# A new order of all steps, and new PSUM pairs, for a fused recurrence and feed-forward kernel on one core

## The chip, the cores and the metric

The kernel runs on one core of one Trainium2 chip. The metric is the time of one execution in microseconds of device time (us); lower is better. The kernel before was run three times: 1061.87, 1062.71 and 1066.75 us, so its median is 1062.71 us.

## What is computed

The reference is a recurrence over 768 time steps for 4 x 8 heads of size 40, whose output goes through an RMS normalisation and a gated feed-forward layer. All tensors are float32.

```python
for t in range(S):                                   # S = 768, state is 40 x 40 per head
    y[:, :, t] = einsum('bhd,bhde->bhe', r[t], state)
    Sa = einsum('bhde,bhe->bhd', state, a[t])
    state = state * w[t][:, :, None, :] - einsum('bhd,bhe->bhde', Sa, b[t])
    state = state + einsum('bhd,bhe->bhde', v[t], k[t])
x = y as (3072 tokens, 320)
xn = x / sqrt(mean(x * x) + 1e-6) * rms_g
out = (silu(xn @ w_gate) * (xn @ w_val)) @ w_out     # 320 -> 1536 -> 320
```

## The kernel before

The time axis is cut into 24 **chunks** of 32 steps. Each chunk has three stages. `front` (L652) loads the chunk's six inputs, turns them with TensorE, and builds products inside the chunk, level by level (1, 2, 4, 8, 16 steps), in eight PE steps that follow each other through ScalarE (ACT) and VectorE (DVE). `inverse` (L760, and `early_inverse`, L778, for the first four chunks) solves a triangular system on VectorE, in some 60 short instructions, with a round trip through DRAM on either side. `main` (L810) carries the state from chunk to chunk and makes the chunk's output. After every second chunk `feed` (L939) runs one **group** of 256 tokens, 12 groups in all, through the feed-forward layer in 12 slices of the hidden dimension. Its weights come from DRAM again for each group: each slice is one load into one of five buffers `wf`, and a buffer comes free only when the `out` matmuls of the slice that used it are done. Group 0 needs the weights in a narrowed form, which `narrow` (L973) makes in 24 half slices at the start of the kernel, with ScalarE, VectorE and DMAs.

No engine call is made where the stages are written. `Plan.add` (L280) notes each step as a piece with its engine, the pieces that it needs, and the PSUM **room** that it uses. There are 6,028 pieces: 2,858 for DVE, 1,024 for ACT, 905 for PE, 696 for SP (all of them DMA issues) and 545 for POOL (GpSimd; 460 of them DMA issues). A PE piece is 3 to 64 matmul records in the profile. `Plan.issue` (L322) then issues the pieces in the order that the string `ORDER` (L33) gives. A word of it is a number counted from the first piece that has not been issued yet, and a `-` is a **filler**: one 128x128 matmul on the identity (L1015) whose result nobody reads. The string `PAIRS` (L228) says which of three PSUM pairs (two banks each) each of the 499 rooms gets. A room keeps its pair from its first to its last piece, so a pair that is given to a new room also makes that room's first matmul wait for the last reader of the old one. The order is the program's: each engine runs its own pieces in this order and waits at each for what the piece needs. DMA issues stand in it too; the loads of chunks 1 to 23 are issued by POOL, weights, chunk round trips and outputs by SP.

The profile knows most instructions by the line of a helper: L444 is every VectorE operation on tensors, L464, L467 and L470 those of ScalarE, L479 and L476 fills and copies on POOL, L483 every DMA issue, L486 every matmul, L489 every turn (transpose by TensorE) and L1015 the fillers. PE steps carry these names below: `turn`, `gramk` (products inside a chunk), `lower`, `state`, `update`, `score`, `level`, `y0` (stage `main`), and `h64`, `h`, `out` (stage `feed`).

## Time and profile before

| | |
|---|---|
| median of three runs | 1062.71 us |
| the profiled execution: span from first to last instruction | 1060.6 us |
| runs' median less that span | 2.1 us |
| PE busy | 1009.5 us (95%), 23406 matmuls |
| weight loads on PE (they overlap matmuls) | 829.3 us |
| DVE busy | 842.3 us (79%), 2861 instructions |
| ACT busy | 468.1 us (44%) |
| POOL busy | 309.5 us (29%) |
| fillers on PE (302 records, two for each of 151) | 48.0 us |
| DMA | 143.35 MB, 135 GB/s on average |

The profile is one execution on the chip. Busy time is time in which an engine runs an instruction; a gap before an instruction is put down to what ended it. The chain of waits (the work that ended last, followed back from the end) is PE for 72% of the span, DVE for 8% and DMA for 4%.

### The profile page before, as it was taken

Reading aid. Unit: us, or ns where it says so; the run is one execution under the profiler, and the core shown is the slowest. Engines: PE = TensorE matmul, PEld = TensorE weight load, DVE = VectorE, ACT = ScalarE, POOL = GpSimd, SP = SyncE. Lnnn points to the kernel's source line nnn. Section 1 sums busy time; section 2 is a strip of 40 time slices with the busy share of each in tenths; the row PEclk is TensorE's granted clock in tenths of the full one; section 3 lists DMA queues with packets and bytes.
Section 4 is the critical chain, followed back from the end, with each engine's and each line's share of the span. In section 5 each row is a group of like instructions: output and inputs, shape, how many; then the busy total and the mean of one; then the engine's idle time right before and its main releaser. Section 6 shows DMA issues by size and latency. Waiting matters only on the chain.

```text
span 1060.6 us, 53494 instructions
## 1 busy us (share of the span) xinstructions
PE 1009.5 (95%) x23406; PEld 829.3 (78%) x23406; DVE 842.3 (79%) x2861; ACT 468.1 (44%) x1043; POOL 309.5 (29%) x554
## 2 busy tenths in 40 slices
PE   7868999999999999999999999999999999999997
PEld 6767777777888778787778778787777888787875
DVE  8978878776868988898898798989889899787411
ACT  6856666643543534434443444434344443431211
POOL 8824413120532241241233241340331331110000
PEclk9777998999999999999999999999999999999999
DMA  9965458766565483655565555574555555443252
GB/s 168 216 155 133 77 127 207 211 123 178 127 140 126 106 173 96 150 134 125 123 155 129 135 132 114 122 160 119 137 126 126 138 137 138 100 132 102 80 162 68
DMA packets 172457, 143.35 MB, mean 135 GB/s; under 512 B 125504, under 2 KB 143872, under 8 KB 172224
## 3 DMA queue, kind: packets, MB, share of 16 engines
q1 hardware_dynamic: 153856, 116.96, 42.9%
q0 software_dynamic: 16192, 22.64, 12.1%
q8 instruction: 184, 3.01, 1.2%
q10 hardware_dynamic: 2176, 0.33, 0.3%
q14 instruction: 49, 0.40, 0.1%
HBM read 123.86 MB, written 15.99 MB: 132 GB/s over the span
## 4 chain that ended last, share of the span: by engine, by line
PE 72%; DVE 8%; DMA 4%; ACT 3%; issue 3%; POOL 2%; SPq 1%; DVEq 0%; ACTq 0%; POOLq 0%
PE ps L486 50%; PE po L486 13%; PE ps L489 8%; DMA wf<-sW 2%; DVE LT L444 1%; DVE y L444 1%; DVE tmp L444 1%; POOL kbn L483 1%; DVE Yi L444 1%; DVE K L444 1%; SPq L483 1%; DMA sY<-Yi 1%; ACT VU L467 1%; PE po L1015 0%; DVE Ab L444 0%
## 5 line engine op out<-in xcount | busy, mean ns | idle before, releaser
L486 PE MATMUL ps<-xg,wf 128*128 128x256 f32 (+1 forms) x1728 | 353.5, 390 | 4.0 <-DVE xg L444 2.0
L486 PEld LDWEIGHTS ps<-xg,wf 128*128 128x128 f32 (+1 forms) x1728 | 261.4, 188 | 57.2 <-issue 15.0
L486 PE MATMUL po<-wf,hT 128*128 128x320 f32 x576 | 183.1, 449 | 0.1
L464 ACT ACTIVATE sg<-ps 128x256 f32<-128x256 f32 x144 | 53.6, 382 | 228.2 <-PE ps L486 224.9
L444 DVE TENSOR_TENSOR tmp<-Yi,M 128x60 f32<-128x60 f32 (+24 forms) x620 | 130.7, 211 | 19.1 <-DMA M<-sB 5.9
L444 DVE TENSOR_TENSOR Yi<-Yi,tmp 128x60 f32<-128x60 f32 (+24 forms) x620 | 129.7, 209 | 12.7
L483 POOL DMA_DIRECT2D VU<-in_v_dram x92 | 53.2, 584 | 274.1 <-PE ps L486 141.8
L486 PEld LDWEIGHTS po<-wf,hT 128*128 128x128 f32 x576 | 102.5, 191 | 35.7 <-issue 4.1
L444 DVE TENSOR_TENSOR hT<-ps,sg 128x256 f32<-128x256 f32 x144 | 59.7, 420 | 67.2 <-ACT sg L464 66.4
L444 DVE TENSOR_TENSOR K<-K,T 128x512 f32<-128x512 f32 (+1 forms) x192 | 93.4, 496 | 8.3 <-PE ps L486 5.8
L486 PEld LDWEIGHTS ps<-Ab,K 40*64 40x64 f32 x4608 | 77.2, 138 | 28.1 <-issue 10.5
L467 ACT COPY K<-K 128x256 f32<-128x256 f32 (+1 forms) x168 | 71.7, 443 | 58.4 <-PE ps L486 39.2
L486 PE MATMUL ps<-Ab,K 40*64 40x56 f32 x4608 | 87.2, 224 | 9.7 <-issue 3.8
L444 DVE TENSOR_TENSOR As<-ps,msi 128x256 f32<-128x256 f32 (+1 forms) x186 | 78.9, 476 | 14.4 <-PE ps L486 13.8
L467 ACT COPY KN<-ps 128x640 f32<-128x640 f32 x96 | 66.1, 690 | 53.5 <-PE ps L489 23.3
L483 POOL DMA_DIRECT2D kbn<-in_b_dram x92 | 53.3, 583 | 96.7 <-PE ps L486 94.3
L486 PEld LDWEIGHTS ps<-As,KN 128*40 128x40 f32 x3072 | 66.5, 124 | 15.7 <-issue 10.4
L483 POOL DMA_DIRECT2D kbn<-in_k_dram x92 | 53.6, 585 | 82.7 <-PE ps L486 82.6
L486 PE MATMUL ps<-As,KN 128*40 128x32 f32 x3072 | 73.2, 205 | 3.1 <-issue 2.5
L483 POOL DMA_DIRECT2D wn<-in_w_dram x92 | 51.6, 567 | 62.7 <-DVE tmp L444 24.1
L444 DVE TENSOR_TENSOR y<-y,ps 128x256 f32<-128x256 f32 x119 | 50.0, 420 | 16.2 <-PE ps L486 13.7
L444 DVE COPY_PREDICATED LT<-near,ps 128x384 f32<-128x384 uint32 (+2 forms) x72 | 52.2, 725 | 2.6 <-PE ps L486 2.0
(133 smaller groups left out, 1546.0 us busy)
## 6 DMA issues: line engine op xcount, KB each, us to landing
wf<-sW SPq DMA_DIRECT2D x144, 480.0 KB, 3.9
M<-sB SPq DMA_DIRECT2D x80, 128.0 KB, 4.1
rn<-in_r_dram SPq DMA_DIRECT2D x24, 160.0 KB, 5.4
sW<-ex SPq DMA_DIRECT2D x16, 240.0 KB, 3.4
out_dram<-o SPq DMA_DIRECT2D x48, 80.0 KB, 4.2
kbn<-in_k_dram POOLq DMA_DIRECT2D x92, 40.0 KB, 3.9
kbn<-in_b_dram POOLq DMA_DIRECT2D x92, 40.0 KB, 4.1
wan<-in_a_dram POOLq DMA_DIRECT2D x46, 80.0 KB, 4.9
```

What stands on the lines that cost most here:

```text
L444: plan.add("DVE", kind, lambda at: fn(at(o), *m(at)), [o], aps(*args))
L464: plan.add("ACT", "act", lambda at: nc.scalar.activation(at(o), at(a), f, **kw), [o] + aps(acc), [a])
L467: plan.add("ACT", "copy", lambda at: nc.scalar.copy(at(o), at(a)), [o], [a])
L483: plan.add(by, "dma", lambda at: queue.dma_start(out=o, in_=i), [o], [i])
L486: return o, lhsT, rhs, lambda at: nc.tensor.matmul(at(o), lhsT, rhs, start=start, stop=stop, skip_group_check=True)
L489: return o, i, ident, lambda at: nc.tensor.transpose(at(o), i, ident)
```

## The change

Only the two strings differ; every piece, its instruction and its operands are the same, and so are the numbers of pieces (6,028), fillers (151) and rooms (499). The new `ORDER` and `PAIRS` come from a search by local exchanges that judged an order by the mean of three draws in which transfers land late.

```diff
 ORDER = """
-85 83 84 76 58 78 86 74 73 59 60 75 5 89 61 88 77 4 43 6 201 7 87 334 90 44 8 214 213 53 62 9 - - - - - - - - 93 18 10
...
+86 5 4 6 7 - 8 9 10 11 12 13 14 15 16 17 58 59 43 19 - 20 - 25 18 38 42 76 85 83 79 73 74 84 75 78 87 77 88 93
+94 - 95 96 100 101 108 111 21 557 558 559 124 112 - 22 26 113 23 24 121 125 568 577 566 578 588 569 589 567
...
 PAIRS = """
-0120112210001221012012210211000102102120201021100221210111012202202000111100112120100012102221212201000112001120122221
...
+01201021120012121120211201020000012020101000212222212101110101200020001111011121202222100200122222011221010121
...
```

Read as orders of each engine, the two differ nearly everywhere, but seldom by much. If the pieces of an engine are laid end to end with the durations of the trace of before, a DVE piece stands 3.6 us of DVE work away from its old place on average, an SP piece 2.7, an ACT piece 2.3 and a POOL piece 4.3. Which stages follow each other, and which chunk runs beside which group, is as before, and both orders end in the same four `out` steps. The three pairs serve 179, 166 and 154 rooms before and 164, 169 and 166 after.

## The prediction

> **What bounds the kernel now.** I read the page's rows of busy time and of the 40 slices first, then busy time by stretch, then the waits of PE, then stretches of the timeline.

> ```profile
> PE 1009.5 (95%) x23406; PEld 829.3 (78%) x23406; DVE 842.3 (79%) x2861; ACT 468.1 (44%) x1043; POOL 309.5 (29%) x554
> ...
> PE   7868999999999999999999999999999999999997
> ...
> DVE  8978878776868988898898798989889899787411
> ...
> PEclk9777998999999999999999999999999999999999
> ```

> The slices are 26.5 us each. From the seventh on PE is full. Before that neither PE nor its clock is. Stretches of busy time give sizes (length, PE, PEld, DVE, ACT, POOL, granted clock, DMA share, GB/s):

> ```profile
> 0.00:20.00 20.00, 14.18 (x246) 13.55 (x250) 15.65 (x48) 9.76 (x19) 18.60 (x43) 1.00 1.00 176
> 20.00:40.00 20.00, 14.78 (x344) 12.61 (x336) 18.62 (x40) 17.92 (x37) 17.46 (x39) 0.82 0.84 174
> 40.00:60.00 20.00, 18.42 (x360) 16.68 (x362) 19.66 (x71) 17.16 (x36) 11.30 (x22) 0.76 0.88 205
> 60.00:80.00 20.00, 13.24 (x354) 11.80 (x347) 13.37 (x47) 9.21 (x19) 2.98 (x7) 0.76 0.67 163
> 80.00:100.00 20.00, 17.64 (x653) 15.85 (x655) 16.95 (x58) 10.70 (x23) 8.74 (x16) 0.73 0.55 146
> 100.00:160.00 60.00, 56.20 (x1734) 47.67 (x1733) 47.32 (x137) 39.28 (x88) 21.29 (x39) 1.00 0.50 100
> 160.00:200.00 40.00, 38.28 (x843) 31.64 (x842) 33.90 (x119) 27.87 (x60) 8.68 (x15) 0.91 0.76 205
> 200.00:600.00 400.00, 390.48 (x9071) 317.25 (x9063) 327.70 (x1143) 169.81 (x388) 122.44 (x209) 1.00 0.58 138
> 600.00:1000.00 400.00, 391.18 (x9460) 320.15 (x9458) 337.51 (x1177) 157.79 (x357) 97.48 (x167) 1.00 0.53 126
> ```

> There are two regimes. Up to 100 us PE is idle for 21.7 us, while DVE is the busy one between 20 and 60 (38.3 of 40) and POOL before 40 (36.1 of 40). From 200 to 1000 PE is busy 781.7 of 800 us: the steps that PE does there set the end, and an order can gain only what PE loses between steps. All PE idle time there is 18.3 us, so large gains are out of reach.

> How PE's time depends on order shows in the timeline (start, length, operation):

> ```profile
> 726.84 1.89 PE L486 MATMUL ps<-xg,wf 128*128 128x256 f32 x8
> 728.66 0.83 PE L486 MATMUL ps<-VU,KN 64*40 64x40 f32 x64
> 729.29 1.12 PE L486 MATMUL ps<-rE,vut 40*64 40x32 f32 x64
> 730.23 1.14 PE L486 MATMUL ps<-Ab,K 40*64 40x56 f32 x64
> 731.30 0.92 PE L489 MATMUL ps<-ident,ST 104*104 104x104 f32 x8
> ```

> A step counts from its start to the next start. An `h` step (first row) takes 1.82 us here, ahead of a step whose weights have another shape; ahead of one of its own shape the least is 1.73. `gramk` (fourth row) takes 1.07 ahead of a turn and 0.97 ahead of `update`. I call such a change of shape a switch.

> **The change part by part.** Nothing is added or removed, so each term is a count from the two orders times a size from this trace.

> *Switches.* Sorted by shape (full 128 rows with turns; `h64`; 64x64; `level`; `lower`; `state`), neighbours on PE differ 532 times before and 497 times after; from group 1 on, where PE is the bound, 414 and 381. Over all pairs after 200 us, a step ahead of a switch takes 0.121 us more than its least, one without 0.063 (stalls over 0.5 us left out). So 33 fewer switches are 33 x 0.058 = 1.9 us; by the least values (0.10) 3.3. I take **-2.0**; ends 0 (the wait merely moves) and -3.3.

> *Short leads.* For each PE step I took the PE work between it and the earlier PE step whose result reaches it through other engines (a freed PSUM pair counted too), less the measured durations of those other steps. Before, of 759 steps from group 1 on, 16 have a lead under 0, 135 under 1 us, 254 under 3, 354 more. Their measured lateness is 0.417, 0.080, 0.035 and 0.052 us each, 44.9 in all. After, the counts are 2, 120, 252 and 385: 0.8 + 9.6 + 8.8 + 20.0 = 39.2, so 5.7 less. But 18.4 us fall on steps with leads over 3 us, late for another reason (queues of DVE and ACT, which the new order mixes anew). I take **-3.5**; ends 0 and -5.7.

> *Weight loads.* A load waits for the `out` step that frees its buffer, so its lead is the PE work from there to the slice's first matmul.

> ```profile
> DMA to landing us min/median/max: 2.0/4.0/9.3
> ```

> Leads under 5 us fall from 4 to 1 and the shortest grows from 3.9 to 4.8; those under 10 rise from 27 to 33. At the median landing all are covered: 0. If the six added short leads met the slowest landing they would cost at most 6 x (9.3 - 4.8) = 27 us, in practice a fraction; this goes to the range.

> *Fillers.* The count is the same, but 8 of the 151 move behind group 0, where PE has no time to spare: 8 x 0.22 = 1.8 us unless they stand in a wait. I take **+0.9**.

> *The start.* POOL is the queue to look at. The last load of chunk 1's k and b stood behind 15.9 us of POOL work and was issued at 17.7; now fills and copies that were needed later stand ahead of it, and it is behind 27.1, so it is issued at 28.9. It lands 3.9 us later by the median row, 6.4 by its own case:

> ```profile
> kbn<-in_k_dram POOLq DMA_DIRECT2D x92, 40.0 KB, 3.9
> ```

> So it lands at 32.8 to 35.3; turn, copy and `gramk` (1.08 + 1.0 + 1.16) give 36.0 to 38.5, where DVE by its own order wants the result at 34.0. DVE waits 2.0 to 4.5 us, and its whole queue with it. Against that stand 1.4 us that DVE idled there anyway, and an order that ends the first elimination 1.8 us of DVE work sooner: net -1.2 to +1.3 at 60 us. Behind that the DVE order brings main of chunk 0 3.8 us forward on average, the `hT` that feeds group 0's eighth `out` 3.8 and chunk 5's `front` 2.8. I take **-1.5** (ends -4 and +5, the latter for a wait of 4.5 that nothing gives back). The chunk 0 loads and round trips on SP move by 1 us on average, and the load that the first elimination waits for is 6 us of SP's order earlier: nothing. The tail is the same: nothing.

> Sum: -2.0 - 3.5 + 0.9 - 1.5 = **-6.1 us**. The span of 1060.6 becomes 1054.5; with the 2.1 us that lie between the profiled span and the runs' median, 1056.6.

> **The rivals.**

> 1. *No change.* Stalls change places: DVE, at 0.83 busy from 200 on, gets a new queue order, and its lateness (18.4 us on steps with long leads) grows by what the short leads give. For it: the weight loads' leads, on which late transfers act, have not grown. Against it: the counts of short leads fall in each class. Time: switches alone, less the fillers, 1061.6.

> 2. *A colder, later start; slower than before.* The granted clock is 0.73 to 0.82 from 20 to 100 us, and a `gramk` that takes 1.16 us at full clock takes 1.98 at half. The new order has 104 fillers rather than 111 ahead of group 0, none rather than 3 (and a `lower`) between chunk 1's first and second `gramk`, and 2 rather than 11 just ahead of the first `inv` step, where PE already idles 4.2 us. If the half clock lasts on through 100 to 160 us, where PE is busy 56.2 of 60, each microsecond of it loses half: 36 us more at half clock cost 18, and the time is 1062.7 - 6.1 + 18 = 1075. It decides against the kernel once more than 23 us are added (11.4 us lost, 1068). Against it: the clock was low between 80 and 100, where PE had 17.6 of 20 busy, so fillers do not govern it alone. [...]

> 3. *More.* Start and short leads give their full ends: -3.3 - 5.7 + 0 - 4 = -13, or 1049.7.

> **How the numbers follow.** Forecast 0.50, at 1056.6, reaching from 1052 to 1062; no change 0.20; slower start 0.18; more 0.12. I take 0.5% (5.3 us, limits 1057.4 and 1068.0) as what a measurement can tell from no change. Faster: 0.30 of the forecast's 0.50 and all of the 0.12, 0.42. Within: 0.20 of the forecast and 0.17 of the first rival, 0.37. Slower: 0.18 and 0.03, 0.21. The range reaches from 1048 (below rival 3) to 1070: it leaves out most of rival 2 and little else. The forecast's own range is 1052 to 1062.

> **What would show it.** PE busy from 200 to 1000 nearer to its clean sum, and the same work ended earlier: group 1's last `out`, 308 us before, should end at 305 or less, and from there to the end another 3 to 5 us should be gained. On POOL the load named above lands at 33 to 35 us and DVE waits ahead of chunk 1's first masked copy. It would be wrong if groups 1 to 11 take as long as before, if a weight load ends many PE waits, or if the granted clock is low past 100 us.

## The result and the profile after

The changed kernel took 1131.07 us (median of four runs, 1123.89 to 1137.86) against 1062.29 us for the kernel before beside it: a ratio of 1.0625, 95% interval 1.0549 to 1.0701. So it is 69 us slower where the prediction said 6 us faster. The profiled execution took 1137.86 us, its span is 1136.1. Now and then a run lies over 1.5% above the fastest of its kernel; in what follows it counts in the median and not in the ratio.

The page of the kernel after: busy time, and PE, DVE and the granted clock in 40 slices of 28.4 us.

```profile
PE 1036.5 (91%) x23406; PEld 849.6 (75%) x23406; DVE 843.9 (74%) x2861; ACT 459.7 (40%) x1043; POOL 309.6 (27%) x554
...
PE   6878887998998999899999899998989999998998
...
DVE  7878676856867787788888789867878879886321
...
PEclk8779997999998999999999999999989999999999
```

PE's row is no longer full from the seventh slice on; eights stand between the nines to the end. The clock dips as late as the 30th slice. DVE is busy for as long as before (843.9 and 842.3 us), so the same work takes longer: something holds PE up. The same stretches as in the prediction (length, PE, PEld, DVE, ACT, POOL, granted clock, DMA share, GB/s):

```profile
0.00:20.00 20.00, 11.66 (x182) 10.73 (x182) 16.50 (x45) 10.66 (x19) 18.04 (x47) 1.00 0.83 174
20.00:40.00 20.00, 14.25 (x276) 13.46 (x280) 14.09 (x34) 12.60 (x26) 14.26 (x28) 0.79 0.65 142
40.00:60.00 20.00, 16.91 (x366) 15.36 (x358) 19.24 (x62) 15.22 (x33) 9.07 (x18) 0.70 0.76 168
60.00:80.00 20.00, 15.30 (x416) 13.98 (x418) 17.27 (x62) 11.26 (x25) 5.05 (x11) 0.73 0.77 209
80.00:100.00 20.00, 17.02 (x557) 15.33 (x549) 11.63 (x37) 11.49 (x22) 6.39 (x14) 0.84 0.43 91
100.00:160.00 60.00, 53.07 (x1688) 44.82 (x1687) 44.62 (x140) 38.41 (x88) 20.57 (x37) 0.97 0.43 94
160.00:200.00 40.00, 32.39 (x626) 26.32 (x628) 27.49 (x89) 17.30 (x36) 11.92 (x21) 0.83 0.63 164
200.00:600.00 400.00, 372.72 (x8530) 303.96 (x8522) 308.37 (x1068) 163.49 (x378) 109.17 (x184) 0.97 0.53 129
600.00:1000.00 400.00, 377.82 (x8991) 307.87 (x8995) 328.46 (x1149) 153.96 (x360) 109.55 (x187) 0.97 0.50 123
```

From 200 to 1000 us PE is busy 750.5 us, before 781.7, and it does 17,521 matmuls there, before 18,531. The last `out` of group 0 ends at 254.6 us (before 238.7), of group 1 at 332.5 (308.4), of group 6 at 764.4 (711.5), of group 11 at 1131.3 (1055.1). So 16 us are lost by group 0 and some 5.5 us in each group behind it: no single place.

What ends PE's idle time (engine, line, tile; total us, times, longest), before and then after:

```profile
PEld ps L486 <- issue: 62.4, 157, 2.0
...
PE ps L486 <- issue: 16.9, 25, 1.8
```

```profile
PEld ps L516 <- issue: 94.9, 167, 3.8
...
PE ps L516 <- issue: 38.0, 39, 3.6
```

"issue" is idle time for which the profile shows no cause, neither a semaphore nor a DMA. It has grown most. On the timeline of PE after (start, length, operation, idle time ahead of it) it looks like this:

```profile
394.73 0.73 PE L516 MATMUL ps<-Ab,K 40*64 40x56 f32 x33
397.44 0.69 PE L516 MATMUL ps<-Ab,K 40*64 40x56 f32 x31 [1.99 <-issue]
398.06 1.99 PE L516 MATMUL ps<-xg,wf 128*128 128x256 f32 x8
```

This is one `gramk` step of chunk 9, 64 matmuls on the same two tiles, broken for 2 us between its 33rd and its 34th matmul. Nothing that the profile sees (a semaphore, a DMA, another engine) ends the wait.

What can, by these traces, is the supply of instructions. The row of the DMA queues is the same in both kernels but for the share, 1.2% before (queue, kind, packets, MB, share):

```profile
q8 instruction: 184, 3.01, 1.1%
```

Each packet has 16384 bytes. PE's part of the trace holds some 47,150 instructions (a matmul record comes with a weight load; 335 are waits on semaphores), which is about 184 times 256. That makes 64 bytes for each, and the packets come from 17.7 to 1118.6 us of the span (before 15.6 to 1043.7): PE's own program is brought in while it runs, in **blocks** of 256 instructions. A block is 128 matmul records with their weight loads, or two `gramk` steps. Numbered from the first instruction in the trace, the long waits without a cause lie at one and the same place of these blocks: of 51 gaps over 0.75 us between the starts of weight loads after 200 us, 22 (36.6 us) end with instruction 190 to 198 modulo 256, nearly all at 193 or 194. Before it was 9 of 21 (10.3 us), at the same two numbers. I call this place the **cut**. The gaps elsewhere have grown as well, from 12 with 11.5 us to 29 with 38.5.

The packets tie the gaps at the cuts to the supply. Of the 22 gaps there, 21 end 1.2 to 1.6 us after a packet of this queue has come in; of the 29 gaps elsewhere, only two do. The n-th packet starts 1.1 (before) and 1.3 us (after) behind the n-th cut in the median, and in neither trace does PE pass the next cut before that packet has come in: the least distance from its end to that cut is 1.2 us before and 0.9 after.

**The theory**, read from these two traces: behind a cut PE has one block in hand, asks for another, and must have it before the first is used up. Where PE waited over 0.75 us at a cut after 200 us, the cut ahead lay 3.1 to 6.0 us back (5% to 95%; median 4.7; 31 waits in the two kernels). Small steps use up a block faster: two `gramk` steps take 1.9 us. For each block I sum the clean durations of its steps and count what it lacks to 3.6 us, the **shortfall**: 14.9 us over all blocks after 200 us before, 31.9 after. The 3.6 us are the median in the trace of before from the start of a packet to the use of its block (3.8 after). They hold time in which a block lay ready, so they are a scale and not a measured limit; the medians from a cut to its packet (1.1), of the packet (1.1) and from its end to the end of a long gap (1.4) happen to add up to the same. The rivals: late transfers with the weights' leads, the queue orders of DVE and ACT, and the start with its fillers and clock.

To size it, I compared every interval between weight loads after 200 us with the clean duration of its step. The excess is *cut* (over 0.2 us, at instruction 190 to 198), *others* (over 0.2 us at a step's start, where its last operand from DVE, ACT or a DMA has just come) or *rest* (changes of shape, half clock, small things):

| us after 200 us | before | after | difference |
|---|---|---|---|
| cut | 14.4 | 41.2 | +26.8 |
| others | 19.1 | 35.9 | +16.8 |
| rest | 15.4 | 35.3 | +19.9 |
| sum | 48.8 | 112.3 | +63.5 |

The clock is in the rest: before it is never at half between 200 us and the end of the last `out`, after it is for 51.2 us in twelve stretches. Nine of them stand behind waits at a cut, three (at 236.5, 478.9 and 1048.9 us) behind gaps of 2.7 to 3.3 us elsewhere.

### The profile page after: what moved, and what is told of

Its sections match the earlier page's. It is cut to its first block, busy times and chain, and to the rows that moved or that the text cites. A ratio compares the mean times of both kernels' runs of the same rounds, so it can differ in the third digit from the quotient of the medians.

```text
span 1136.1 us, 53417 instructions
## 1 busy us (share of the span) xinstructions
PE 1036.5 (91%) x23406; PEld 849.6 (75%) x23406; DVE 843.9 (74%) x2861; ACT 459.7 (40%) x1043; POOL 309.6 (27%) x554
## 4 chain that ended last, share of the span: by engine, by line
PE 67%; DVE 15%; issue 6%; DMA 5%; ACT 3%; POOL 2%; SPq 1%; DVEq 0%; ACTq 0%; POOLq 0%
PE ps L516 45%; PE po L516 12%; PE ps L519 8%; DVE LT L474 2%; PE po L1045 2%; DVE tmp L474 2%; DVE Yi L474 2%; DVE K L474 2%; POOL kbn L513 2%; DVE y L474 2%; SPq L513 1%; DVE Ab L474 1%; DMA M<-sB 1%; DVE hT L474 1%; DMA sB<-LT 1%
## 5 line engine op out<-in xcount | busy, mean ns | idle before, releaser
L516 PE MATMUL ps<-xg,wf 128*128 128x256 f32 (+1 forms) x1728 | 363.0, 402 | 0.9 <-DVE y L474 0.9
L516 PEld LDWEIGHTS ps<-xg,wf 128*128 128x128 f32 (+1 forms) x1728 | 268.4, 195 | 54.2 <-issue 15.1
L516 PE MATMUL po<-wf,hT 128*128 128x320 f32 x576 | 185.5, 456 | 5.9 <-issue 3.9
L516 PEld LDWEIGHTS po<-wf,hT 128*128 128x128 f32 x576 | 106.9, 198 | 41.4 <-issue 8.3
L516 PE MATMUL ps<-Ab,K 40*64 40x56 f32 x4608 | 89.7, 227 | 25.1 <-issue 9.3
L516 PEld LDWEIGHTS ps<-Ab,K 40*64 40x64 f32 x4608 | 79.7, 140 | 42.8 <-issue 20.6
L474 DVE TENSOR_TENSOR As<-ps,msi 128x256 f32<-128x256 f32 (+1 forms) x186 | 80.3, 475 | 19.7 <-PE ps L516 18.1
L516 PEld LDWEIGHTS ps<-As,KN 128*40 128x40 f32 x3072 | 65.4, 124 | 21.3 <-issue 13.9
L503 POOL TENSOR_TENSOR ss<-ss,mhalf 128x1 f32<-128x1 f32 x24 | 16.2, 674 | 189.5 <-DVE ss L474 188.6
```

Of the source, the lines that this page charges most:

```text
L474: plan.add("DVE", kind, lambda at: fn(at(o), *m(at)), [o], aps(*args))
L503: plan.add("POOL", "tt", lambda at: nc.gpsimd.tensor_tensor(o, a, b, op), [o], [a, b])
L516: return o, lhsT, rhs, lambda at: nc.tensor.matmul(at(o), lhsT, rhs, start=start, stop=stop, skip_group_check=True)
```

## The experiments

**Instructions put ahead of an unchanged order.** A filler is split into two of half the width: the same columns, but four more instructions (two matmuls of two records, each with a weight load, in place of one). The cuts move through the whole program; apart from the split fillers themselves, all of them ahead of group 0, nothing else does. The number of split fillers is 32, 4, 36, 16, 48, 16 and 52 in the seven runs.

```diff
-    plan.warm = lambda: nc.tensor.matmul(po_[:, 0, DM:DM + P], ident, ident, start=False, stop=False, skip_group_check=True)
+    filler = lambda lo, hi: nc.tensor.matmul(po_[:, 0, DM + lo:DM + hi], ident, ident[:, lo:hi], start=False, stop=False, skip_group_check=True)
+    def warm():
+        fillers[0] += 1
+        for lo, hi in ((0, 64), (64, P)) if fillers[0] <= 32 else ((0, P),):
+            filler(lo, hi)
+    plan.warm = warm
```

> The kernel before, with its first 32 fillers each issued as two of 64 columns in place of one of 128: the same order everywhere and the same columns of work, but 128 more instructions in TensorE's stream (a matmul is four: two passes of a weight load and a matmul) ahead of group 0. Theory (TensorE starves for instructions): the traces show TensorE's stream fetched in packets of 16384 bytes (184 of them in both kernels, 256 instructions each), a median of 3.6 us from asking for one to its use, and the stalls of both kernels at one and the same place of these blocks (instruction 193 of 256). Blocks of small matmuls are used up in less than 3.6 us of clean time; after 200 us these shortfalls add up to 14.9 us in the kernel before and 31.9 us in the kernel after. Moved by 128 instructions the blocks of the kernel before are cut elsewhere, and the shortfalls add up to 33.6 us: so 30 to 75 us slower (1090 to 1135), with most of the loss inside TensorE steps. Rivals (fillers and clock at the start, late transfers, pairs and order of VectorE and ScalarE): nothing of theirs is changed, so 1060 to 1068.

> The kernel before, with its first 4 fillers each issued as two of 64 columns: 16 more instructions ahead of group 0. Theory: the shortfalls of the blocks add up to 14.4 us after 200 us in place of 14.9, so the time stays within 6 us of the kernel before (1057 to 1068). Together with the run of 128 it tells whether the place of the blocks matters or any change of the fillers. Rivals: the same, 1060 to 1068.

> The kernel after, with its first 36 fillers each issued as two of 64 columns: 144 more instructions ahead of group 0. Theory: the shortfalls of its blocks add up to 43.3 us after 200 us in place of 31.9, so slower still than after, by 10 to 40 us (1140 to 1170). Rivals: as the kernel after, 1124 to 1138.

> The kernel before with its first 16 fillers each issued as two of 64 columns: 64 more instructions ahead of group 0, the order unchanged. The shortfalls of the blocks below 3.6 us after 200 us are 27.5 us at this place, against 14.9 at the kernel's own and 33.6 at 128 (which took 1117). Theory (the place of the cuts): 1090 to 1115. Rival (128 was unlucky, the order is robust): 1060 to 1080.

> The kernel before with its first 48 fillers each issued as two of 64 columns: 192 more instructions, the order unchanged. Shortfalls 31.7 us. Theory: 1095 to 1120. Rival (128 was unlucky): 1060 to 1080.

> The kernel after with its first 16 fillers each issued as two of 64 columns: 64 more instructions, the order unchanged. Shortfalls 40.1 us, against 31.9 at its own place and 43.3 at 144 (which took 1154). Theory: 1125 to 1155; the changed order is slow at every place. Rival (after's own place is unlucky): below 1100.

> The kernel after with its first 52 fillers each issued as two of 64 columns: 208 more instructions, the order unchanged. Shortfalls 35.9 us. Theory: 1120 to 1150. Rival (after's own place is unlucky): below 1100.

Measured (the ratio is to the kernel before on the same chip, 1066.2 to 1066.6 us there; the kernels' own places head the two halves):

| order, instructions ahead | shortfall | us | ratio, 95% interval | cut | others | rest |
|---|---|---|---|---|---|---|
| before, 0 | 14.9 | 1062 to 1067 | 1 | 14.4 | 19.1 | 15.4 |
| before, 16 | 14.4 | 1077.5 | 1.0099 (1.0065 to 1.0134) | 13.7 | 18.6 | 15.9 |
| before, 64 | 27.5 | 1105.0 | 1.0363 (1.0303 to 1.0424) | 38.8 | 18.7 | 22.2 |
| before, 128 | 33.6 | 1116.6 | 1.0479 (1.0413 to 1.0545) | 42.0 | 20.5 | 38.7 |
| before, 192 | 31.7 | 1113.2 | 1.0433 (1.0375 to 1.0492) | 44.4 | 20.0 | 27.5 |
| after, 0 | 31.9 | 1131.1 | 1.0625 (1.0549 to 1.0701) | 41.2 | 35.9 | 35.3 |
| after, 64 | 40.1 | 1145.7 | 1.0740 (1.0670 to 1.0810) | 48.2 | 36.4 | 41.0 |
| after, 144 | 43.3 | 1154.1 | 1.0760 (1.0661 to 1.0860) | 48.2 | 36.2 | 40.0 |
| after, 208 | 35.9 | 1145.7 | 1.0708 (1.0612 to 1.0804) | 42.0 | 36.3 | 45.0 |

Six of the seven came out within the theory's range and outside the rivals'. For the kernel after this says less, since the intervals of its ratios at the three new places overlap with that at its own. The waits of the kernel before with 128 instructions ahead (the same two rows):

```profile
PEld ps L486 <- issue: 91.0, 169, 3.5
PE ps L486 <- issue: 39.7, 35, 3.4
```

With an order that has not changed in any queue, they have the size of the kernel after, and they still begin at 193 and 194 of a block, so at other steps. The column "others" hardly moves with the place (18.6 to 20.5 and 35.9 to 36.4): it belongs to the order. The miss is 16 instructions: after 200 us the loss is as expected (48.3 us, before 48.8), but group 0 ends at 250.2 us instead of 238.7. The start is sensitive too (251.3, 255.0 and 247.8 with 64, 128 and 192), and the shortfall, counted after 200 us, does not cover it. Whether the cuts or the split fillers delay the start was not told apart.

**The supply alone.** A kernel that only issues matmuls: 8 sets of 4 large ones, 80 steps of the shape of `gramk`, 40 large sets, and 80 steps again, with 60 loads of 480 KB running beside their first part. It was run once.

```diff
+        gramk(80)
+        large(40, xg)
...
+        for load in range(60):
...
+            nc.sync.dma_start(out=wf[load % 5].bitcast(I32), in_=src[load % 2 * P:load % 2 * P + P, 960 * (load % 3):960 * (load % 3) + 960])
+        gramk(80)
```

> Leaves the reference's work out: it only issues matmuls, and writes zeros. 80 steps of the shape of gramk (32 small matmuls, 128 instructions) with nothing else running, then 40 sets of 4 large ones, then 80 steps of gramk while SP loads 60 tiles of weights. Theory: clean, a step of gramk takes 0.97 us, so a block of 256 instructions 1.9 us, and 80 of them 78 us; if a block can't be had faster than every 3.6 us, the run of gramk takes about 140 us with a stall in each block, and longer or not while the loads run (the fetch's share of the queues). If only latency counts and several fetches may be under way, about 78 us. Rivals need 78 us in both.

Three stretches: small matmuls alone, with the loads, and behind them (length, PE, PEld, DVE, POOL, clock, DMA share, GB/s):

```profile
60.00:100.00 40.00, 39.09 (x1403) 37.87 (x1400) 0.00 (x0) 0.00 (x0) 0.50 0.02 5
260.00:300.00 40.00, 25.10 (x884) 23.88 (x880) 0.00 (x0) 0.00 (x0) 0.50 1.02 404
320.00:360.00 40.00, 39.47 (x1408) 38.08 (x1405) 0.00 (x0) 0.00 (x0) 0.50 0.02 5
```

128 matmul records with their weight loads are a block, so a block takes 40 x 128 / 1403 = 3.65 us alone and 40 x 128 / 884 = 5.8 us beside full DMA queues, with 2.1 to 2.9 us of it waited at instruction 193 of each block (3.9 in the first). No instruction here depends on the loads. The first 80 steps took 146.7 us, near the theory's 140, but the clock stood at half, at which PE by itself needs nearly that (it was busy for 39.09 of 40 us): a match by luck, and 3.65 us is only an upper bound for the idle machine. The clock had fallen to half at 23.7 us, at the end of a gap of 2.7 us at a cut. It stayed there for 146.8 us, though PE was busy for 39.1 of 40, and came back at 170.5 us, 4.9 us after the large matmuls had begun. The 5.8 us is the supply's own: at the same clock PE was idle for 14.9 of 40 us beside 404 GB/s, and for 0.9 beside 5 GB/s.

**Less traffic.** The reloads of the weights are left out from the 18th on, in both kernels, so later groups multiply by old weights.

```diff
-                dma(wf, sW[f + e])
+                dma(wf, sW[f + e], skip=FT * g + f + e >= FT + WB)
```

> The kernel after without the reloads of the weights: the first 17 loads of wf (group 0, and one for each of the five tiles) stay, the other 127 are left out, so the later groups multiply by old weights; every other instruction and order stays. It takes some 62 of the 117 MB off SP's queue. Theory: a block of instructions took 3.65 us with the queues empty and 5.8 us with them full where the fetch was run alone, so with less traffic fewer blocks run out: the waits at instruction 193 after 200 us fall from 41 to 15 to 25 us, and the time to 1085 to 1115. Rival, late transfers of weights as the cause of the loss: down to the kernel before or below, at most 1070, with the same waits at instruction 193. Rival, other engines' orders or the clock: 1120 to 1138.

> The kernel before without the same 127 reloads of weights (left out as in the run of after). Theory: its 14 us of waits at instruction 193 after 200 us fall to about 7, so 1040 to 1060; the gap between the two kernels shrinks from 69 to 35 to 60 us. Rival, late transfers of weights as the cause: 1062 and a gap near nothing.

After fell to 1095.25 us (1.0301, 1.0227 to 1.0376), before to 1060.48 (0.9939, 0.9905 to 0.9973): the gap is 35 us. The rows of waits of the kernel after without reloads:

```profile
PEld ps L516 <- issue: 73.8, 147, 5.2
...
PE ps L516 <- issue: 21.3, 24, 5.1
```

Cut fell from 41.2 to 16.8, rest from 35.3 to 16.7 (half clock 10.2 us), others stayed (36.6). Before: 11.4, 16.3 and 20.2; its waits at cuts fell less than expected (to about 7), and its time lies at the edge of the theory's range. So late weights were not what held the kernel after: without them its waits for others are as they were. What fell with the traffic were the waits at cuts and the half clock, and half of the 69 us goes with them.

**TensorE's order rearranged.** Steps of PE are exchanged within a few places so that no block is short; judged by a model with the trace's durations and the supply of instructions. The first, second and fourth change PE's order alone, the third those of all engines. A piece of the first, as PE's steps in order, named by stage, number and kind (an excerpt):

```diff
 main9.turn
+feed3.out
 front11.gramk
+feed3.h64
+feed3.h
 main9.y0
-feed3.h64
 main9.score
-feed3.h
```

> The kernel after with TensorE's order alone rearranged: 459 of its 905 steps move, most by one place and none by more than seven, so that no block of 256 instructions is made of small steps only; the orders of the other four queues, the pairs, the fillers and the start stay those of the change. The shortfalls of TensorE's blocks below 3.6 us after 200 us fall from 31.9 to about 9 us, and the shape switches rise from 470 to 517. Theory (TensorE starves for instructions): most of the loss comes back, 1035 to 1080. Rivals: a cause in the orders of VectorE, ScalarE, POOL or SP, in the pairs, or in the fillers and the start is untouched, so 1115 to 1140; a loss by switches or leads of TensorE's own would grow.

> The kernel before with TensorE's order alone rearranged in the same way: 404 of its 905 steps move, most by one place and none by more than nine. The shortfalls of its blocks fall from 14.9 to about 6 us; shape switches 512 to 523. Theory: faster than the kernel before by 10 to 40 us (1022 to 1055), since the kernel before also starves in places. Rivals: the kernel before doesn't starve, so 1055 to 1075.

> The kernel before with the orders of all five engines moved by local exchanges, judged by when TensorE's blocks run out beside the waits for other engines (439 steps of TensorE by at most eight places). The shortfalls fall from 14.9 to about 7 us. Theory: faster than the kernel before by 10 to 40 us (1022 to 1055), about like the rearranged TensorE order alone. Rivals: what moves on the other engines decides, so as likely slower than the kernel before as faster.

> The kernel before with TensorE's order alone rearranged (451 steps, by at most ten places) so that blocks are not short wherever they are cut: the shortfalls are 8 to 22 us over all places of the cuts, against 15 to 35 in the kernel before, at the price of 39 more shape switches (512 to 551). Theory: 1035 to 1065, and little change if instructions are put ahead of it. Rivals: slower by the switches alone, 1062 to 1075.

| run | us | ratio, 95% interval | cut | others | rest |
|---|---|---|---|---|---|
| after, PE rearranged | 1151.2 | 1.07 (two runs), no interval | 16.7 | 65.9 | 40.0 |
| before, PE rearranged | 1122.7 | 1.0546 (1.0468 to 1.0624) | 20.9 | 53.3 | 32.2 |
| before, all rearranged | 1251.0 | 1.1748 (1.1655 to 1.1840) | 21.3 | 122.2 | 51.9 |
| before, for any place | 1140.2 | 1.0709 (1.0639 to 1.0780) | 19.7 | 64.2 | 22.3 |

All four missed, and the third agrees with its rival, that what moves on the other engines decides. The first did what it was made for at the cuts, and the time did not come back: PE now waits for results. The rows of its waits:

```profile
PEld ps L488 <- issue: 63.0, 145, 2.5
PEld ps L488 <- ACT K L469: 16.3, 22, 1.8
...
PE ps L488 <- issue: 16.6, 18, 2.4
```

The issue rows are back at the size of before, and a wait for ACT of 16.3 us stands beside them (4.2 in the kernel after). In the kernel before, the rearranged orders did not even lower the cut: 20.9 and 19.7 for 14.4. So the shortfall tells what moving the cuts does to a given order; it did not tell which order would be good. And the leads for other engines, which the model took at clean durations, are worth more than it had them at.

**A few steps only.** Where the trace shows a wait at a cut, the next step whose operands had long landed is put ahead of the held one: 16 moves by one to five places in the kernel after, 6 in the kernel before. One of the 16:

```diff
 feed3.out
+feed3.h
 main9.update
 front11.gramk
-feed3.h
 main9.turn
```

> The kernel after with 16 steps of TensorE moved, each by one to five places, and nothing else changed: at 16 of the 44 places where its trace shows TensorE held at instruction 193 of a block, the next h, h64, out or turn whose operands had long landed is put ahead of the held step, so that the wait is filled with work that came later anyway. Theory (TensorE starves for instructions): the 16 waits hold 22 us, of which 16 us are filled, and some of the half clock that follows them goes with them: faster than the kernel after by 10 to 25 us (1106 to 1121). It differs from the rearrangement of 459 steps in that no lead of another engine gets shorter. Rivals (other engines' orders, pairs, fillers): 1124 to 1138.

> The kernel before with 6 steps of TensorE moved by one to three places in the same way, at 6 of its 24 such waits (20 us in all). Theory: 5 us filled, so 1052 to 1062 and, if it holds, faster than both kernels; if the cuts of later blocks move with them, up to 15 us slower. Rivals: no change, 1060 to 1068.

After: 1132.68 us (1.0665, 1.0581 to 1.0750), no better than without the moves and within the rivals' range. Cut fell from 41.2 to 28.0, others rose from 35.9 to 42.8, rest from 35.3 to 38.5; the sum went from 112.3 to 109.3. Before: 1068.46 (1.0020, 0.9986 to 1.0054), no change. What was filled at the cuts was mostly waited elsewhere, more than half of it for DVE, ACT and DMAs. No version that does all the work beat the kernel before.

## Why the prediction was wrong, point by point

**What bounds the kernel.** "The steps that PE does there set the end, and an order can gain only what PE loses between steps": this held for gains. It was read as if losses were bounded too. 18.3 us of PE idle time was all there was to gain, while nothing bounded what a new order could lose. The prediction spread 44.9 us of lateness over classes of leads, and put the 18.4 us of it on long leads down to the queues of DVE and ACT. It took times from step to step and did not look inside steps. The trace of before held 14.4 us of waits at cuts after 200 us, and most of the long ones stand inside a step, as in this row of before, 27 matmuls of a `gramk` held up behind 37, at instruction 193 of a block:

```profile
361.50 0.67 PE L486 MATMUL ps<-Ab,K 40*64 40x56 f32 x27 [0.57 <-issue]
```

This is the failed step: the sum had no term for where the cuts of PE's instruction stream fall, and any rearrangement moves steps across them. In its place the runs showed waits at cuts of 41.2 us (14.4 before), with 51.2 us of half clock. The second failed step is the sign of the short leads, below.

**Switches** (-2.0): right. Steps after 200 us lose 69.4 us to excesses below 0.5 us, before 72.8, at nearly the same prices (0.123 and 0.065, before 0.121 and 0.063). That is 3.4 us gained, the term's end. The excesses over 0.5 us grew from 21.6 to 89.4.

**Short leads** (-3.5): wrong in sign. Waits for others rose by 16.8 us although the counts of short leads fell in each class. They do not move with the place of the cuts (35.9 to 36.4 at four places, against 18.6 to 20.5), so they are the order's own. The prediction's doubt, that DVE's new queue order may make its results later, was right; its size was not seen from PE's leads. The traces show where much of it lies. Of the 29 gaps over 0.75 us away from cuts, seven (14.9 us) end with VectorE's product `hT` of a group; before it is one of 12 (1.2 us). None of the steps that wait there reads `hT`: each is the first of a room whose PSUM pair `hT` was the last to read. So these steps wait for a pair to come free. Whether the new `PAIRS` or the new order is to blame was not run apart.

**Weight loads** (0): right. PE's waits on DMAs in the kernel after are 4.5 us after 200 us, for inputs of `front` that POOL loads, and leaving the reloads out did not lower the waits for others.

**Fillers** (+0.9): too small to be told apart.

**The start** (-1.5): group 0 ended 15.9 us later. The load on POOL landed at 31.8 us and chunk 1's first masked copy ran at 38.5 instead of 33.5: 5.0 us later, about the far end of that term. By the last `level` step of chunk 0's and 1's `main` the kernel is only 5.6 and 3.4 us late, by chunk 3's 14.8. That part can come from the cuts, since the unchanged order ends group 0 9 to 16 us late too when they move; it was not told apart further.

**The rivals.** The slower one had the right sign with another cause. Half clock did last past 100 us (17.1 us of it from there to 200, before 6.8), but behind waits of PE, and the bulk of the loss came later. The range ended at 1070.

**How much is the place.** Over four places each, some 64 instructions apart (0, 64, 128, 192 and 0, 64, 144, 208), the mean ratio to the kernel before is 1.032 for the old order and 1.071 for the new one. So 41 us are the orders' own. Behind 200 us the same means of the table's columns differ by 10 us in cut, 17 in others and 14 in rest. The kernel before stands 34 us below the mean of its places and the kernel after 9 below its own: 41 + 34 - 9 = 66 of the 69 us. The good place of the kernel before is gone 64 instructions away. Whether it came by luck or was picked when that kernel was made, no run here can tell.

**What stays open.** Why the results of DVE and ACT come later in the new order was traced only as far as the freed pairs above. Some blocks of under 2 us passed without a wait, so the moment at which a block is asked for is not known exactly.

**The clock.** In the kernel after half clock set in at 345.7, 362.8 and 755.3 us behind gaps of at most 2.0, 1.5 and 1.5 us between weight loads, and lasted 3.4 us each time. Gaps of 2.3, 2.5 and 2.1 us at 397, 518 and 907 us passed without it, so in this trace the length of one gap did not decide alone.

## What to carry to other kernels

Before judging an order of small matmuls, count how fast each run of 256 TensorE instructions is used up (here the waits came behind blocks that took 3.1 to 6.0 us from cut to cut, wait included, and a block took 5.8 beside 404 GB/s of loads), and look for steps that stop in the middle with no cause. A tuned order may owe much of its time to where these cuts fall (here 1062 us at the order's own place, 1077.5 to 1116.6 at four others): shift it by some instructions and measure before comparing two orders, or the comparison is one of places. A count of leads at clean durations did not forecast how late other engines would be once their own queues were reordered (waits for them: 3.5 us less forecast, 16.8 more measured).
